# Rounded matrix products whose moving operand is read as two interleaved streams

## The chip, the cores and the metric

The kernel runs on one core of one Trainium2 chip. The metric is device time of one execution in microseconds (us), lower being better. A core has TensorE for matrix products (PE in the rows, with its weight loads as PEld), VectorE (DVE), ScalarE (ACT), GpSimd (POOL) and SyncE (SP), whose queue issues all of this kernel's transfers.

## The reference

What is computed is causal attention with a decay bias, for 8 batches of 8 heads, 576 tokens and 64 features a head, and a gated MLP on the concatenated heads:

```python
scores = q @ k.T / 8                                   # (8, 8, 576, 576)
cum = np.cumsum(np.maximum(s, 0.0), axis=-1)
scores = np.where(causal, -1e9, scores + np.minimum(-(cum[..., :, None] - cum[..., None, :]), 0.0))
attn = np.exp(scores - scores.max(-1)); attn /= attn.sum(-1) + 1e-9
x = heads_concatenated(attn @ v)                       # (8, 576, 512)
h = gelu_tanh(x @ w_in)                                # (8, 576, 1024)
u, v = h[..., :512], h[..., 512:]
v_n = (v - mean(v)) / sqrt(var(v) + 1e-6) * g_ln
v_s = einsum('ts,bsd->btd', w_sg, v_n) + b_sg[None, :, None]
out = x + (u * v_s) @ w_out
```

All tensors are float32.

## The kernel before

Everything is one stream of small instructions that the program first records and then issues in a fixed order: each call goes through a recorder (class `Plan`), and a table of ranks (`RANK`, a packed string) sets the place of every operation on its engine. So all rows of the profile have the recorder's line, and operations are told apart by tile names. A second set of tables (`ALT`, with `ENG` as the default) says for each copy, split and scaling whether ACT (`s`), POOL (`g`) or DVE (`v`) does it. Engines run their own queue strictly in that order.

Products. Most run as rounded float32 (float32r): an operand is split into a rounded high part and a low rest, and a product is the sum of three products (high with high, high with low, low with high) in the same PSUM bank. Each matmul instruction loads 128 columns of weights (the stationary operand) and then streams the columns of the moving operand past them.

- Keys (`qk_part`, tiles `pss<-k,q`): for the 56 heads from number 8 on, the moving operand is a stretch of the split keys `k1`, `k2`; per head two instructions each of 448, 64, 320 and 192 columns and four of 288. Rows 64 and 65 of `k2` hold the running sum `cum` of the bias, brought from a scratch tensor in DRAM. The first 8 heads use unrounded float32 (tiles `kq`, `arena`).
- MLP, for each of 8 batches: `v_unit` (tiles `psm<-wi,xs`, 512 columns of the weights `wi` move; 56 instructions a batch), `u_unit` (`psm<-xs,wi`, 288 token columns of `xs` move; 8 units of 12), `s_unit` (`psm<-ws,vn` and `psm<-wr,vnr`, 288 columns of `ws` move; 8 units of 14), `o_unit` (`psm<-gt,wo`, 288 columns of `gt` move; 8 units of 12). Some go to banks named `pss` or `psp`.
- Transposes of the attention matrix (`psp<-ident,p`) and context products (`psp<-pT,vf`) in unrounded float32.
- At the start `WARM` and `FILL` instructions, which multiply a single column of ones, broadcast to 512 columns (`psm<-wt`), keep TensorE occupied.

Evictions. `gelu2` reads a unit's PSUM bank three times: ACT squares it, DVE reads it twice. The end of `o_unit` reads it once on DVE and adds the residual `xr`. In the key part, `split_k` turns the loaded `raw` into `k1` (copy, `kh`) and the rest (subtraction, `kl`), and SP then moves pieces between partitions.

Of the kernel before, what the change touches and what calls it, by code (L numbers as in the profile page):

```python
# [12 lines left out]
F32 = mybir.dt.float32  # L13
# [52 lines left out]
ENG = dict(kh="s", kl="g", xh="g", xl="g", gh="s", gl="g", wh="s", wl="g", wsh="s", wsl="gggv", n="g", vl="g", ev="s",  # L66
# [4 lines left out]
    "na": "sgggggssgvvgsggsssggvgggsgsggggg",  # L71
    "wh": "svsvsgggsggg",
    "wl": "gggggggggggg",
    "ea": "vvvssvss",
    "xva": "vsss",
    "xa": "ggsgsgss",
    "xal": "gggggggg",
    "nb": "ggsggsggsgssggggggvgvggg",
    "eb": "ssssssss",
    "eb1": "ssssssvv",  # L80
    "xvb": "sssv",
    "rt": "ggvvvggggvgvgvvvgvggvgvvggvvgvggvggvvvvvvvgggggvgvgggggvggvgggggvvgggvvggvgvvvgv",
    "vl": "gggggvgggvggvvgvgvvgggvvgggggggg",
    "kh": "sgsssssvgggvsssggvggvgvgvvsvsgssgssgsgsggvsvsssgssvgggvg",
    "kl": "gggggggvvggggvvgggvvvvgvgggggggvggggvvgvvvvgvvvgvvggggvg",
    "wsh": "sssssssssvsv",
    "wsl": "gggggggvgggg",
    "n": (
        "ggggggvggggggggggggssvggsggssggsssgvgsggsgssgvvsvvgvsgsggvvgsgsvgsvssvvvgssgsggvgsggsgsssssgsgsgvgss"
        "ggvgssggvgggvssgvggsvgvvgsvvsgggvgsssggggssgsgvvgsvgsvgggsgssvgggvsssgvggvggsvvvvgsssgsgsvvssvvvvvgv"  # L90
        "gvvvgvgggsgggssvggggvsvsgsgsgvssvvsvsgsvvvvsggsssgvgggsgsggsssssggvgsgvggssggvggssssvggssgggsgvsvvss"
        "gggsggvvvsgsgvggggggsvggsvsggssgvvsgssvgvvsvvvvsvvggvvsgvvggsggssggssggggssggssssvgsggvggvvg"),
    "ev": (
        "ssvsvsvvvssssvsvssvsssvsssssvsssvsssvvvsvsvvssssvssvsvvsvsssssvsssssssssssssssvvssvsvvssssvsvssvsssv"
        "svsvvvssvvvs"),
    "ev1": "sssvssvsvsvvvvvssssvssssvsvvsvsvssvsvssvssvssvvsssvvsvss",
    "xv": "vsvvvssvssvsvsvsvvsssvssvsvv",
    "xw": "svsvvvvsssssvssvssvvvsssssvs",
    "xz": "sssssvssvvsvsvsvsvsvvvsvsssv",
    "gh": "vgvggvvsgvgssvsggsgsvvsvgvvvgsggvgggvsssgsgsvssgsvgggssgvsvsgggv",  # L100
    "gl": "vvgvvvggvgvvggvgvvgvgvgvgvvvvgggggggggggggggggvggggggggggggvvggv",
    "xh": "ssvssssvgggssvssssssssgvsvvs",
    "xl": "vggvvvvggggggvvvgggvvvvvvgvv",
# [15 lines left out]
    "To!H%H-xXk6XA;hL`U2z>=W(_?}eMf17W4GMz||H6@Cc61wj-=T~x#x!V&?BMTIlMdEt}rU68~;48_FaA>oqnO86|i6MhMgh1bG20f}5pB&HVAh#AC8;yvNHkWS1l"
    "78KtK{{%xMA`=scy@V}-CYmA@<BF-o^kQZ)ub4y3BQ_KM2(svjk(g2}Am$VcizP)@Od`$}vWmIILSkvLf>=$gDApHN3;D$oVqLL=kX`sI)Dr87EyS*3e{rbzLD(<s"  # L120
    "6dH@I#L_}OvA9@9%q12P&k09`Q$i}CoLEJyFSZuji=D-uVkfbII9{ACE)pAwrNl~NbuqcvR~#aa6{m>v#7$xov9{P$Y%U%XJ_>JymSP*RoKREjAa)Z6iX+5v;v{jD"
    "*hQQ#t`gUX-NkldZ!t#fCvFx8h`q$YVpXxBI7mD!4iis_7saDutT<AfAkGn2itEHZ;#P5tI8mG{E*4jd+r{1D0r7;mOFS=L7vqVQ#be?*@xJ&*{3Ze^zIa@`Azl#^"
    "io?ZO;s!CPI9XgMrV!hT&BQEXQSqv{T-+h<70-%K#dqRs@uOHw{3Rkul}3vz#Es%kahe!NGsOMkNpZHAL|P`U6}O4|#3SMv@t*ix{32cxe~P|zLChwW7kh}0#l+Gf"
    "@v?YZd?|hw|A@9ENKeExQYPt{m_SM;WszQqm&9A*L-DP6Q+y$|6W)uT#IIrs>4*4F^du(5k&;P?r1;WbQIRYOOI(U4C6&@j>7{H^ekp@gQ)(hLl<tUk#mrJ+sigEk"
    "d?cDuD8-dTDVbPSOe<y->xdo2nPO#0l61+DWGS)GNNOWNsj1XT(j-H2rPNYZDYsNksv^~rYD*0yB2g)l5=tqhj8bc9kTgQ-BD9b?NZF-MQeP>j)J#e)<&fG+xuhCm"
    "9;twoS1K(Pm5NLKg$h!2sf1KYDkN2v>PY>i;nEmshBR3!BbAk^N%f?bQah==v{+gzZIU`lQ^h6X0&%IhUOXtC7C(purD9TNX^+%Z>Lt~ex=6#MKGGzqo77y2mF7qT"
    "rEyXZsi$;K>MivV(@FWHB2szjn6v{7kbaAmq{h-<DMlJ9jhDWQ-KDA0JZZVKMfxWVk<LhCrMc2lX@j&~x+dL|_DQ>?3({d}uQXFyA{~-0N+YE$;wY(xv{Bk29gt2)"
    "C&71cReCComL^F3r2EoqX`-}Fx+y)AK1$!Eta532iZo4{E`5;F0tNh%>Pq{ilhOidg|tjsEp3$!O1GuW(rjssv`acJot9QgN2K%8dTE<fQ93H!k<LojrCHKtX})wy"
    "dL+G-zDj>24`c?(L1K^wFpv-|lom-lrB%{9>5C+ROOg$~Nx4BG@KE|I)dwNy0Io<kq+8Nm>4EfEdLq4)-b*he1LOo1!2^(5ehG5OucZ8-G^hqDfH%@}>9h1(`Xm7m"
    "7bF2cBoXK!0P#UekOdS3H9#|v5A*;7fech201OfU7sLSwv;ZdfDRGbjK;Qri_<#TkA`lNG0_j0gkPM^(*+CId4m1ayKp)Tzv;)&Xd(a<b1%*K=P#H7?twAr)7YqVj"  # L130
# [1279 lines left out]
def _layout(i):  # L1410
# [9 lines left out]
    def bits(a):  # L1420
        return np.ascontiguousarray(a).view(np.int64) if a.dtype == np.float64 else a
# [39 lines left out]
```

## Time and profile before

| | |
|---|---|
| time, median of 3 runs | 736.41 us (735.29 to 737.32) |
| time of the profiled execution | 735.24 us |
| span in its profile, first to last instruction | 733.5 us |
| TensorE busy | 725.5 us, 99% |
| VectorE, ScalarE, GpSimd busy | 582.0 us (79%), 501.7 us (68%), 367.4 us (50%) |
| granted TensorE clock | 1.000 of full speed on average |

The profiled execution is 1.7 us longer than its span and 1.2 us shorter than the median. A matmul's duration in the rows contains a tail that overlaps the next instruction: many of 288 columns last 299 ns each and start every 133 ns. A rate is therefore read from a run of like instructions in the timeline: the time of the run, less one duration, over one instruction fewer.

### The profile page before, as it was taken

The page shows a single profiled execution, that of the slowest core. Times are in us where ns is not written, and L with a number is a line of the kernel's source. Part 1 is how long each engine was busy: PE and PEld are TensorE (multiplying, and loading weights), DVE is VectorE, ACT ScalarE, POOL GpSimd, SP SyncE. Part 2 cuts the span into 40 slices and gives each one's busy share as a digit, 9 for nine tenths or more (in the row PEclk, how much of TensorE's full clock was granted, in tenths as well). Part 3 has the DMA queues.
Part 4 walks back from the last instruction along what each step waited for, and adds up shares of the span by engine and source line. Part 5 has one row for each costly group of instructions (what it writes and reads, how often), then busy time and mean ns, then how long its engine had stood idle before and what let it go on. Part 6 is the DMA issues. An engine that isn't in the chain of part 4 may idle for free.

```text
span 733.5 us, 16206 instructions
## 1 busy us (share of the span) xinstructions
PE 725.5 (99%) x5337; PEld 641.5 (87%) x5337; DVE 582.0 (79%) x1761; ACT 501.7 (68%) x1378; POOL 367.4 (50%) x604
## 2 busy tenths in 40 slices
PE   8999999999999999999999999999999999999998
PEld 7877789988889888898889898998889888889998
DVE  6898988799887779779897588867898777965663
ACT  5899986777986567855686687866788555931430
POOL 6899897444663344733343263363535454541621
PEclk9999999999999999999999999999999999999999
DMA  8974744555454453353443544434445343100101
GB/s 250 273 197 130 179 124 120 157 142 149 124 157 119 119 136 96 94 155 107 132 123 83 152 122 110 112 96 128 128 132 132 103 120 107 44 9 24 49 17 65
DMA packets 59272, 88.35 MB, mean 120 GB/s; under 512 B 16306, under 2 KB 33972, under 8 KB 59188
## 3 DMA queue, kind: packets, MB, share of 16 engines
q1 hardware_dynamic: 59188, 87.32, 43.5%
q8 instruction: 42, 0.69, 0.4%
q14 instruction: 42, 0.34, 0.2%
HBM read 41.37 MB, written 9.73 MB: 70 GB/s over the span
## 4 chain that ended last, share of the span: by engine, by line
PE 92%; DVE 3%; DMA 2%; ACT 1%; issue 1%; POOL 1%; SPq 0%; DVEq 0%; ACTq 0%; POOLq 0%
PE psm L451 54%; PE psp L451 21%; PE pss L451 16%; DVE p L451 1%; DMA pair<-in_w_in 1%; DMA q<-k 1%; DVE psm L451 1%; DMA k<-cum 0%; POOL p L451 0%; DMA vf<-in_vp 0%; ACT p L451 0%; SPq L451 0%; DVE u L451 0%; DVE vt L451 0%; POOL wi L451 0%
## 5 line engine op out<-in xcount | busy, mean ns | idle before, releaser
L451 ACT ACTIVATE p<-p,mn 128x448 f32<-128x448 f32 (+4 forms) x310 | 172.4, 557 | 49.2 <-DVE mn L451 47.1
L451 DVE CUSTOM_DVE_ANT_0 p<-pss,mask 64x64 f32<-64x64 f32 (+4 forms) x304 | 123.0, 424 | 24.2 <-PE pss L451 20.7
L451 POOL TENSOR_SCALAR p<-p,rs 64x64 f32<-64x64 f32 (+4 forms) x199 | 94.9, 486 | 67.3 <-DVE rs L451 51.5
L451 PE MATMUL psm<-gt,wo 128*128 128x288 f32 x720 | 124.1, 299 | 0.0
L451 PE MATMUL pss<-k,q 128*128 128x288 f32 (+9 forms) x672 | 121.1, 297 | 0.5 <-DVE mn L451 0.4
L451 PE MATMUL psm<-xs,wi 128*128 128x288 f32 x720 | 119.0, 300 | 0.9 <-DVE u L451 0.8
L451 PE MATMUL psm<-ws,vn 128*128 128x288 f32 x708 | 117.4, 298 | 0.0
L451 PEld LDWEIGHTS pss<-k,q 128*128 128x128 f32 (+3 forms) x672 | 102.0, 180 | 9.4 <-DVE mn L451 0.8
L451 PEld LDWEIGHTS psm<-gt,wo 128*128 128x128 f32 x720 | 105.1, 188 | 2.5 <-DVE u L451 0.2
L451 PE MATMUL psm<-wi,xs 128*128 128x512 f32 (+1 forms) x380 | 106.4, 402 | 0.0
L451 PEld LDWEIGHTS psm<-xs,wi 128*128 128x128 f32 x720 | 102.0, 188 | 2.6 <-DVE u L451 1.1
L451 PEld LDWEIGHTS psm<-ws,vn 128*128 128x128 f32 x708 | 101.0, 188 | 1.0
L451 PE MATMUL psp<-pT,vf 128*64 128x64 f32 (+3 forms) x752 | 90.4, 388 | 0.6 <-DVE pT L451 0.6
L451 PEld LDWEIGHTS psp<-pT,vf 128*64 128x64 f32 x752 | 46.6, 137 | 43.7 <-issue 30.5
L451 ACT COPY pT<-psp 128x512 f32<-128x512 f32 x124 | 68.8, 580 | 15.4 <-PE psp L451 15.0
L451 PEld LDWEIGHTS psm<-wi,xs 128*128 128x128 f32 (+1 forms) x380 | 66.6, 184 | 12.9 <-issue 0.6
L451 PE MATMUL psp<-ident,p 128*128 128x128 f32 x744 | 72.4, 247 | 0.0
L451 PEld LDWEIGHTS psp<-ident,p 128*128 128x128 f32 x744 | 70.2, 140 | 2.5 <-issue 0.6
L451 ACT ACTIVATE p<-p,rs 64x64 f32<-64x64 f32 (+4 forms) x138 | 62.8, 475 | 11.0 <-DVE rs L451 7.1
L451 POOL TENSOR_TENSOR k<-raw,k 128x576 fp32r<-128x576 f32 x34 | 48.6, 1430 | 29.0 <-DVE k L451 14.4
L451 POOL TENSOR_TENSOR gt<-u,gt 128x288 fp32r<-128x288 f32 (+1 forms) x44 | 37.4, 854 | 48.5 <-DVE gt L451 25.5
L451 DVE SCALAR_TENSOR_TENSOR u<-u,psm 128x288 f32<-128x288 f32 x120 | 52.5, 442 | 10.1 <-ACT u L451 9.6
(158 smaller groups left out, 1208.2 us busy)
## 6 DMA issues: line engine op xcount, KB each, us to landing
q<-k SPq DMA_DIRECT2D x168, 144.0 KB
raw<-in_kq SPq DMA_DIRECT2D x56, 288.0 KB
vf<-in_vp SPq DMA_DIRECT2D x56, 192.0 KB
out_t<-u SPq DMA_DIRECT2D x64, 144.0 KB
k<-k SPq DMA_DIRECT2D x56, 144.0 KB
pair<-in_w_in SPq DMA_DIRECT2D x8, 512.0 KB
u<-xs SPq DMA_DIRECT2D x32, 64.0 KB
pair<-in_w_out SPq DMA_DIRECT2D x4, 512.0 KB
```

What stands on the lines that cost most here:

```text
L451: fn(*args, **kw)
```

## The change

The moving operand of every rounded product is read through a pattern of three levels, in which the innermost level has two elements far apart: column 0, then column n/2, then 1, then n/2+1 (`woven`), and for keys the same inside groups of eight columns (`woven8`: 0, 4, 1, 5, 2, 6, 3, 7). Where the data comes from DRAM it is stored there in the order that makes the products come out straight: keys in groups of 8, the v half of `w_in`, the columns of `w_sg` and `b_sg`. Where the data is made on the chip (`xs` in `u_unit`, `gt` in `o_unit`), the columns lie interleaved in PSUM, and the readers of PSUM go through it with a step of two (`plain`) and write the two halves apart (`halves`). A second running sum, `cum8`, is made in the order of the keys by one more copy (`c8`) and one more transfer to DRAM; the first 8 heads go on reading `cum`.

The planner's price of a rounded product with such a pattern changes, and the ranks and the tables of engines are new.

```diff
+ENG = dict(c8="g", kh="s", kl="g", xh="g", xl="g", gh="s", gl="g", wh="s", wl="g", wsh="s", wsl="gggv", n="g", vl="g", ev="s",
...
-    "kl": "gggggggvvggggvvgggvvvvgvgggggggvggggvvgvvvvgvvvgvvggggvg",
+    "kl": "gggggggvgggggggggvvggggggggggggvggvggvgggggvggggvvggvggv",
...
+def _view(t, *dims):
+    return bass.AP(t.tensor, t.offset, [list(t.ap)[0]] + [list(x) for x in dims])
+def woven(t):
+    n = _cols(t)
+    return _view(t, (1, n // 2), (n // 2, 2))
+def woven8(t):
+    return _view(t, (8, _cols(t) // 8), (1, 4), (4, 2))
+def plain(t):
+    return _view(t, (1, 2), (2, _cols(t) // 2))
+def halves(t):
+    return t.rearrange("p (a n) -> p a n", a=2)
+def weave(n, k):
+    return np.arange(n).reshape(n // k, k // 2, 2).transpose(0, 2, 1).ravel()
...
-            o.pes.append((max(54.0, 0.836 * w), 0.4397 * n + 6.4, 165.0, 0))
+            fast = list(ins[1].ap)[-1][1] == 2
+            o.pes.append((max(54.0, 0.836 * w), n / 2.4 + 2.6 if fast else 0.4397 * n + 6.4, 165.0, 0))
...
+    c8 = moe.tile([P, S], F32, name="c8", tag="xs", bufs=4)
+    copy("c8", c8.rearrange("p (g b a) -> p g b a", b=2, a=4), _view(cc.bitcast(F32), (8, S // 8), (1, 2), (2, 4)))
+    nc.sync.dma_start(out=cum8.rearrange("a h s -> (a h) s"), in_=c8)
...
-        nc.sync.dma_start(out=k2[64:66, :].bitcast(F32), in_=cum[:, h, :])
+        nc.sync.dma_start(out=k2[64:66, :].bitcast(F32), in_=cum8[:, h, :])
...
-        nc.tensor.matmul(o, d["q1"][:, i0:i0 + r], d["k1"][:, j0:j1], start=True, stop=False)
-        nc.tensor.matmul(o, q2[h % 2][:, i0:i0 + r], d["k2"][0:66, j0:j1], start=False, stop=True)
+        nc.tensor.matmul(o, d["q1"][:, i0:i0 + r], woven8(d["k1"][:, j0:j1]), start=True, stop=False)
+        nc.tensor.matmul(o, q2[h % 2][:, i0:i0 + r], woven8(d["k2"][0:66, j0:j1]), start=False, stop=True)
...
-                        nc.tensor.matmul(ps[0:r], xs[c][:, xi, ts_], wi[:, c, wj, fs],
+                        nc.tensor.matmul(ps[0:r], xs[c][:, xi, ts_], woven(wi[:, c, wj, fs]),
...
-                    nc.tensor.matmul(ps[:, 0:CH], wi[:, c, wj, dt * P:(dt + 1) * P], xs[c][:, xi, cs],
+                    nc.tensor.matmul(ps[:, 0:CH], wi[:, c, wj, dt * P:(dt + 1) * P], woven(xs[c][:, xi, cs]),
...
-            gelu2(ps[:, 0:CH], t)
+            gelu2(plain(ps[:, 0:CH]), halves(t))
...
-                    nc.tensor.matmul(ps[:, 0:CH], vn[j][:, vi, ds_], ws[:, j, wj, cs],
+                    nc.tensor.matmul(ps[:, 0:CH], vn[j][:, vi, ds_], woven(ws[:, j, wj, cs]),
...
-                    nc.tensor.matmul(ps[:, 0:CH], wo[:, c, wj, ms], gt[ch, c][:, gi, :],
+                    nc.tensor.matmul(ps[:, 0:CH], wo[:, c, wj, ms], woven(gt[ch, c][:, gi, :]),
...
-            nc.vector.scalar_tensor_tensor(out=t, in0=ps[:, 0:CH], scalar=0.5, in1=xr[(b, mt)][:, cs],
+            nc.vector.scalar_tensor_tensor(out=halves(t), in0=plain(ps[:, 0:CH]), scalar=0.5, in1=halves(xr[(b, mt)][:, cs]),
...
-    kq = np.concatenate([k.transpose(0, 2, 1), q.transpose(0, 2, 1)[:, :, tok]], axis=1)
+    kq = np.concatenate([k.transpose(0, 2, 1)[:, :, weave(S, 8)], q.transpose(0, 2, 1)[:, :, tok]], axis=1)
...
-        "w_in": bits(i["moe_w_in"]),
+        "w_in": bits(i["moe_w_in"][:, np.concatenate([np.arange(DH), DH + weave(DH, DH)])]),
...
-        "w_sgt": i["moe_w_sg"][tok][:, tok].T,
+        "w_sgt": i["moe_w_sg"][tok[weave(S, CH)]][:, tok].T,
```

The new order at three places. The first is the start of SP's queue, in the loads before the first heads: `cum` is the running sum, `xs_86` and `xs_87` the tile that it comes from, `kb`, `ka`, `vp` and `va` are keys, queries and values, `pair` the raw weights. Before:

```order
L451 DMA e_71<-in_va 128x512 x2
L451 DMA g_b_92<-in_g_ln 128x512
L451 DMA cum<-xs_86 128x576
L451 DMA e_71<-in_va 128x1024
L451 DMA pair_121<-in_w_in 128x1024
L451 DMA vf_140<-in_vp 128x320
```

And now:

```order
L481 DMA e_71<-in_va 128x512
L481 DMA arena_80<-in_kb 64x832
L481 DMA cum<-xs_87 128x576
L481 DMA vf_138<-in_vp 128x320
L481 DMA cum_76<-xs_88 128x576
L481 DMA e_71<-in_va 128x1024
```

One transfer of 128x576 is added (`cum_76` is `cum8`, from the copy `xs_88`, which POOL makes), two places behind `cum`; the weights' loads stand elsewhere.

The second place is the split of the keys of head 22. Before, DVE makes the low part (`k_291<-raw_355`) between two score evictions (`ISA p<-pss`) and the statistics of a v unit (`rt`):

```order
L451 SCALAR_TENSOR_TENSOR u_295_367<-u_295_367,psm_65 128x288
L451 ISA p_66,mn_350<-pss_59,mask_18_90,mn_350 128x288
L451 ISA mn_350 128x1
L451 TENSOR_TENSOR k_291_363<-raw_355,k_290_362 128x576
L451 SCALAR_TENSOR_TENSOR rt_360<-rt_360 128x1
L451 TENSOR_SCALAR rt_360<-rt_360 128x1
L451 TENSOR_TENSOR rt_360<-rt_360 128x1
L451 COPY pT_24_96<-psp_61 128x512
```

Now POOL makes the same low part (`k_292<-raw_357`), between scalings of attention rows and that statistics chain:

```order
L481 TENSOR_SCALAR p_68<-p_68,rs_339 64x64
L481 TENSOR_TENSOR k_292_365<-raw_357,k_291_364 128x576
L481 TENSOR_SCALAR rt_362<-mv_361 128x1
L481 TENSOR_TENSOR rt_362<-rt_362,few_93 128x1
L481 TENSOR_SCALAR p_66<-p_66,rs_356 128x320
L481 TENSOR_TENSOR rt_362<-rt_362 128x1 x2
```

Over the whole program the low parts of keys go from 22 on DVE and 34 on POOL to 11 and 45.

The third place is PE's queue at that head's first products. Before, keys of 320 and 192 columns stand between two units of 288 and then come v products of 512:

```order
L451 MATMUL psm_65<-xs_316,wi_99 128x288 x2
L451 MATMUL psm_65<-xs_320,wi_99 128x288 x3
L451 MATMUL pss_59<-k_290_362,q_292_364 128x320
L451 MATMUL pss_59<-k_291_363,q_0_25_97 128x320
L451 MATMUL pss_59<-k_290_362,q_292_364 128x192
L451 MATMUL pss_59<-k_291_363,q_0_25_97 128x192
L451 MATMUL psm_64<-xs_307,wi_99 128x288 x2
L451 MATMUL psm_64<-xs_311,wi_99 128x288
L451 MATMUL psm_63<-wi_99,u_310_382 128x512
```

Now:

```order
L481 MATMUL psm_65<-xs_318,wi_101 128x288
L481 MATMUL psm_65<-xs_322,wi_101 128x288 x3
L481 MATMUL pss_59<-k_291_364,q_293_366 128x320
L481 MATMUL pss_59<-k_292_365,q_0_26_99 128x320
L481 MATMUL pss_59<-k_291_364,q_293_366 128x192
L481 MATMUL pss_59<-k_292_365,q_0_26_99 128x192
L481 MATMUL psm_64<-xs_309,wi_101 128x288 x3
L481 MATMUL psm_64<-xs_313,wi_101 128x288 x3
L481 MATMUL psm_64<-xs_318,wi_101 128x288 x3
```

The kinds, shapes and numbers of TensorE's instructions are the same over the whole program (4867 in the program's list, both times); only what stands beside what has moved.

## Rows read from the trace of the kernel before

**Rows 1.** The page, span and busy time of each engine.

```profile
span 733.5 us, 16206 instructions
...
PE 725.5 (99%) x5337; PEld 641.5 (87%) x5337; DVE 582.0 (79%) x1761; ACT 501.7 (68%) x1378; POOL 367.4 (50%) x604
```

**Rows 2.** The page's chain that ended last, shares by engine.

```profile
PE 92%; DVE 3%; DMA 2%; ACT 1%; issue 1%; POOL 1%; SPq 0%; DVEq 0%; ACTq 0%; POOLq 0%
```

**Rows 3.** Longest wait of PE: tile, releaser, us in total, times, longest.

```profile
PE psm L451 <- DMA kq<-in_ka: 1.6, 1, 1.6
```

**Rows 4.** Windows: us, busy PE, PEld, DVE, ACT, POOL, clock, DMA share, GB/s.

```profile
0.00:20.00 20.00, 17.35 (x87) 14.59 (x88) 14.15 (x50) 10.79 (x34) 13.32 (x31) 1.00 0.89 263
100.00:200.00 100.00, 99.17 (x756) 87.75 (x755) 86.45 (x274) 78.70 (x223) 54.83 (x76) 1.00 0.51 137
200.00:300.00 100.00, 99.74 (x750) 88.60 (x749) 82.78 (x264) 71.72 (x202) 45.55 (x76) 1.00 0.47 127
...
400.00:500.00 100.00, 100.00 (x743) 89.98 (x742) 75.11 (x238) 72.71 (x197) 42.01 (x71) 1.00 0.43 116
```

**Rows 5.** Timeline of PE: start, us to last end, tile, shape, count.

```profile
683.55 1.79 PE L451 MATMUL pss<-wi,xs 128*128 128x512 f32 x7
685.18 3.36 PE L451 MATMUL psm<-gt,wo 128*128 128x288 f32 x24
...
4.73 2.57 PE L451 MATMUL psm<-wt 128*128 128x512 f32 x11
...
275.78 0.27 PE L451 MATMUL pss<-k,q 66*128 66x192 f32 x1
275.89 0.32 PE L451 MATMUL psm<-gt,wo 128*128 128x288 f32 x1
```

**Rows 6.** PE groups by form (last: us 5.1 to 7.0): count, busy us, mean ns.

```profile
L451 PE MATMUL psm<-gt,wo 128*128 128x288 f32 x720 | 124.1, 299 | 0.0
...
L451 PE MATMUL pss<-wi,xs 128*128 128x512 f32 x24 | 6.9, 395 | 0.0
...
L451 PE MATMUL psm<-wt 128*128 128x512 f32 x11 | 2.6, 381 | 0.0
```

**Rows 7.** The chain in order of time, us 414: start, us, what.

```profile
414.09 2.85 PE psp L451 x24
```

**Rows 8.** Groups of DVE and ACT by form that read PSUM.

```profile
L451 DVE SCALAR_TENSOR_TENSOR u<-u,psm 128x288 f32<-128x288 f32 x120 | 52.5, 442 | 10.1 <-ACT u L451 9.6
...
L451 DVE SCALAR_TENSOR_TENSOR u<-psm,xr 128x288 f32<-128x288 f32 x60 | 27.0, 453 | 21.8 <-PE psm L451 21.1
...
L451 DVE SCALAR_TENSOR_TENSOR vt<-vt,psm 128x512 f32<-128x512 f32 x29 | 19.7, 678 | 4.6 <-ACT vt L451 4.5
...
L451 DVE SCALAR_TENSOR_TENSOR gt<-pair,psm 128x512 int32<-128x512 int32 x12 | 8.2, 680 | 0.1
...
L451 ACT ACTIVATE u<-psm 128x288 f32<-128x288 f32 x60 | 24.1, 404 | 23.7 <-PE psm L451 23.4
```

**Rows 9.** Groups of DVE and POOL that split keys.

```profile
L451 DVE TENSOR_TENSOR k<-raw,k 128x576 fp32r<-128x576 f32 x22 | 17.7, 804 | 4.2 <-ACT k L451 4.1
...
L451 POOL TENSOR_TENSOR k<-raw,k 128x576 fp32r<-128x576 f32 x34 | 48.6, 1430 | 29.0 <-DVE k L451 14.4 <-ACT k L451 9.2 <-DMA vf<-in_vp 3.0
...
L451 POOL TENSOR_SCALAR k<-raw 128x576 fp32r<-128x576 f32 x21 | 14.3, 681 | 40.9 <-PE pss L451 33.8 <-DMA k<-k 2.7 <-PE psm L451 1.8
```

**Rows 10.** The chain in order of time, us 79 to 87: start, us, what.

```profile
79.11 4.75 DMA q<-k
...
83.88 2.92 DMA k<-cum
```

**Rows 11.** Timeline of the end: start, us, what, [idle before].

```profile
729.02 1.23 PE L451 MATMUL psm<-gt,wo 128*128 128x288 f32 x8
...
730.28 0.46 DVE L451 SCALAR_TENSOR_TENSOR u<-psm,xr 128x288 f32<-128x288 f32 x1 [0.61 <-PE psm L451]
```

More of the change, by code (lines that the diff above doesn't have):

```diff
@@ L70 @@
     "th": "s",
[L71 to L78, printed above, removed]
+    "c8": "g",
+    "na": "sggsggssgvvgsggggggsvgggsgssgggs",
+    "wh": "sgsgvsgssggg",
+    "wl": "vggvgggggggg",
+    "ea": "svvssvss",
+    "xva": "ssss",
+    "xa": "ggggggss",
+    "xal": "vggggggg",
+    "nb": "ggsggsggssssggvgggvgvggg",
     "eb": "ssssssss",
-    "eb1": "ssssssvv",
+    "eb1": "ssvsssvv",
@@ L81 @@
     "xvb": "sssv",
[L82 to L86 removed]
+    "rt": "gggvgggggvgvvvggggvvvggggggggvggvgvvgvvvgvvvgvgvgvgggggvggvggvgvvggvggvvggvggvgv",
+    "vl": "gggggvgggvggvvvggggggvvvvvvgggvg",
+    "kh": "sgsssssssggsgsssgsggvsvsggsssvvgvgssggvsvgsgvssgggvvggvs",
@@ L102 @@
-    "xh": "ssvssssvgggssvssssssssgvsvvs",
-    "xl": "vggvvvvggggggvvvgggvvvvvvgvv",
+        "ssvsssvvvsvsvsvvssvsssvsssssssssssssvvsvvssvsssssvsvvvsvsvsssssvvsvvssvvsssvsssssvsvvvssssvsvsvsssvs"
+        "svsvssssssss"),
+    "ev1": "ssvvsssssssvvvvvsssssssvvvsssvsvssvvvsssvssssvvssvsvsvsv",
+    "xv": "sssssvssvvssssvvsssvssssvsvs",
+    "xw": "vssvsssvsvvssvsvsvsvvvvsssvs",
+    "xz": "ssvsssvvsvvsssvsssssvssssvvv",
+    "gh": "vssvvsvsgvsssvgvggvssggsgsvvvvsvvggsggssgssssgssvvgsvvgsvgggvvvs",
@@ L104 @@
+    "gl": "vgvgggggvvggggvgvvgggvgvggvggvvggvvvvggvvgvggvgvggvvggvvgggvvvgg",
+    "xh": "sgvvssssgssgvssgsvsgsssgggsg",
+    "xl": "vvgvvggvggvgvvvvgvgvgvggvggv",
 }
@@ L119 @@
[L119 to L130, printed above, removed]
@@ new lines @@
+    "^Nc(*&%(3woIDTD%M0>CyfDA-J@rcS>byR0&MWdtygdKwDcs@_Pr#G%OuQCP#hdb!JU6extMS!d4PKk);%Rv{UWeD?4R~YTgg4`@c?aH`59XuzBtD(b<tz9szLy{2"
+    "{dj*qkPqT9d>r4%XYvJn2p`IaahnG`KKFTIo}ZWC!}$n4nvdZV_+;LWx94qmPaey=^8vgg@60I=c|2a1H{xA*SKf{H;JtVs-j|Q%6ZsUrmha-L`5L~CPvwjFCcc?x"
+    "<y(0xzKU<-hxloJhri?(`DK2CU*I?S4xWtf<a_u&zMmiDC-^mfkH6(#_%Hs4%f97{KKJAM)A$TNo6q6%_<X*QFXl`5Qofvj<k0`kfAW=lJ>Sg_^JRPs-_AGi1N=O{"
+    "%a8J7{5U_!Pw_MSI)A|5@caA;Kg-YY<o+don}6b8x#P$4ukfq<7Jtq^^Y1(jugXXA@tpd$@A|$U_>upPdwyI$fuGb*>8J5C`dR#femTFM-^6d`xAq(Ref%+gtpAWF"
@@ L238 @@
+    "qk2(;sBzRK>Kb*6x<~z@A<=*7d}|>")
 N3 = 8
@@ L1202, in v_unit @@
                     if c < 3:
-                        nc.tensor.matmul(ps, xq[c], wi[:, c, 0, fs], start=(c == 0), stop=False)
+                        nc.tensor.matmul(ps, xq[c], woven(wi[:, c, 0, fs]), start=(c == 0), stop=False)
                         yield W5
-                    nc.tensor.matmul(ps[0:r], xs[c][:, 0, ts_], wi[:, c, 1, fs], start=False, stop=False)
+                    nc.tensor.matmul(ps[0:r], xs[c][:, 0, ts_], woven(wi[:, c, 1, fs]), start=False, stop=False)
                     yield W5
                     if c == 3:
-                        nc.tensor.matmul(ps, xq[c], wi[:, c, 0, fs], start=False, stop=True)
+                        nc.tensor.matmul(ps, xq[c], woven(wi[:, c, 0, fs]), start=False, stop=True)
                         yield W5
@@ L1288, in s_unit @@
                     n += 1
-            nc.tensor.matmul(ps[:, 0:CH], vn[4][:, ds_], wr1[:, cs], start=False, stop=False)
+            nc.tensor.matmul(ps[:, 0:CH], vn[4][:, ds_], woven(wr1[:, cs]), start=False, stop=False)
             yield W2
-            nc.tensor.matmul(ps[:, 0:CH], vnr2[:, ds_], wr2[:, cs], start=False, stop=True)
+            nc.tensor.matmul(ps[:, 0:CH], vnr2[:, ds_], woven(wr2[:, cs]), start=False, stop=True)
             yield W2
```

250 lines of the change are left out of this document (125 added, 125 removed).

## The prediction

> **What bounds the kernel now.** I read the page's busy times first: TensorE is busy 99% of the span, VectorE 79%, ScalarE 68%, GpSimd 50% [rows 1]. A busy TensorE need not be at its peak, so the chain that ended last came next: 92% of it lies on TensorE [rows 2]. Its longest wait for another engine is 1.6 us, at the start [rows 3], and in the windows from 100 us on it is busy 99 to 100 us of each 100 [rows 4]. The exception is the stretch before 87 us, where the chain runs partly through transfers (4.75 and 2.92 us in one place, [rows 10]). So the time is the sum of what TensorE streams, and the question is what a column costs it.
>
> The timeline answers that. Seven products of 512 columns take 1.79 us [rows 5] with a last duration of 0.395 [rows 6]: (1.79 - 0.395) / 6 = 232.5 ns each. Twenty-four of 288 take 3.36 us, the last 0.299: 3.061 / 23 = 133.1 ns. The two widths give the price of a column, 99.4 / 224 = 0.444 ns, and of an instruction, 133.1 - 288 x 0.444 = 5.3 ns. [...]
>
> **The change, part by part.** *Reads in two streams.* From the loops of the program: 8 batches x (96 u + 112 s + 96 o) = 2432 instructions of 288 columns and 224 of keys; 448 of 512; and 112 each of 448, 320, 192 and 64. Together 3552 instructions and 1.109 million columns, so each 0.01 ns of a column is 11 us of the kernel. No row shows a rounded product with such a pattern. [...] The loss side stands under the rivals.
>
> [...]
>
> *Can the weight loads follow?* A full weight load stands before each product. Behind a 192-column key product the next product of 288 starts after 0.11 us [rows 5], so a load needs no more than that; 133 - 10 = 123 ns stays above it. [...]
>
> *Reads of PSUM with a step of two.* 64 u units are read twice by VectorE (442 ns) and once by ScalarE (404), 64 o units once by VectorE (453) [rows 8]. Unknown in PSUM. The nearest rows are VectorE's reads of the raw weights, every second word in SBUF: 680 ns against 678 for the plain form of that size [rows 8]. From above: if each of the 288 elements took a second turn at the rate of those rows ((678 - 442) / 224 = 1.05 ns), 303 ns more, 192 x 0.303 = 58 us of VectorE. I take 0 by the nearest row; VectorE's slack hides some of it, and the upper end is a rival below. At the end, one such read lies bare behind the last product (0.46 us, [rows 11]): 0.3 us at most.
>
> *The second running sum.* One POOL copy of 128x576, 0.68 us by its plain twin [rows 9], and one transfer of 0.29 MB. Behind the copy POOL has memsets, and SP's queue the values and weights of the first heads; the transfers there move 263 GB/s [rows 4], so they come about 1.1 us later. Its reader is head 8, whose running sum lands at 86.8 us now [rows 10]. TensorE's own work for the first heads covers it; without that cover, 1.1 us.
>
> *The new order.* TensorE has the same instructions. Eleven low parts of keys leave VectorE (11 x 0.80 = 8.8 us) for POOL (11 x 1.43 = 15.7 us) [rows 9]; POOL is half idle after 100 us [rows 4] and hides them. What is behind them on POOL is the statistics chain of a v unit and scalings of attention rows, which come up to 1.4 us later and whose readers have other units' products in front of them.
>
> *What is late next.* The other engines must do the same work in 5% less time. VectorE's fullest window, 86.5 of 100 us [rows 4], less 1.2 for the moved keys, becomes 85.3 of 95, 90%. I allow 1.5 us for new waits there and 1.5 for the 28 us or so before 87 us in which the chain is not TensorE's, where about 5% of the stretch is not gained: 3 us.
>
> **Sum.** On the profiled execution's own time: 735.2 - 36.4 + 3 = 701.8 us. The median lies 1.2 above that execution: 703.
>
> **Rivals.** *Each read of a new place waits, and the kernel is slower.* Neighbouring columns of the moving operand now come from two places 576 to 1024 bytes apart (16 bytes for keys). If TensorE's reader holds one piece of SBUF at a time, every column fetches anew what contiguous reading fetched once for several. The start-up row, with no walking at all, doesn't exclude it, and no row has an alternating read. It decides as soon as a column costs above 0.446 ns, 0.5% more than now. At the slowest column of any row, the unrounded context products with 24 instructions over 3200 columns in 2.85 us [rows 7], 0.89 ns, the loss is 1.109 million x 0.446 = 495 us: about 1230 us. [...]
>
> [...]
>
> *VectorE becomes the bound.* With 303 ns more for each of 192 reads, some 30 of them per 100 us, VectorE would have 85.3 + 9.1 = 94 of 95 us in the fullest window and 91 in the next, 83 in the loosest [rows 4]. An in-order engine that full holds up TensorE; if three of six windows lose what they gained (5 us each), 718 us. For it speaks only that no strided read of PSUM is shown; against it, the strided rows of SBUF.
>
> **How the numbers follow.** My forecast, with its own range of 691 (all the fixed part gone) to 710 (none of it, and some more waits): 0.72. VectorE the bound: 0.10, 712 to 726. Nothing in the rate: 0.08. Slower by the reads: 0.10. The range of 692 to 724 holds nearly all of the first and most of the second. About 0.3% either way (2.2 us) is what a measurement of this kernel can tell. Faster: 0.72 + 0.10 + 0.02 of the third case = 0.84; the same 0.05; slower 0.10 + 0.01.
>
> **What will show it.** A run of 24 products of 288 should take 3.14 us (123.6 ns each) and seven of 512 1.70 us; with the fixed part whole 3.18 and 1.71, and with no effect 3.36 and 1.79. The start-up products and the context products must keep their times. The u and o reads should stay at 442 and 453 ns; at 700 or more the third rival is on. TensorE should stay at 98 to 99% of a span near 700, VectorE rise to about 82%. I am wrong if the runs don't shorten, if keys (groups of eight) behave unlike the wide patterns, or if the runs shorten and the windows fill with waits for VectorE.

## The result, and the profile after

| | before | after |
|---|---|---|
| time, median | 736.48 us (4 runs, 735.29 to 737.32) | 709.51 us (4 runs, 707.96 to 709.99) |
| ratio to before | | 0.9631, 95% interval 0.961 to 0.9652 |
| span of the profiled execution | 733.5 us | 707.9 us |

The change takes 27 us away. The forecast was 703, with a range of 692 to 724. The page of the changed kernel, span, busy times and shares of the chain that ended last:

```profile
span 707.9 us, 16218 instructions
...
PE 694.4 (98%) x5337; PEld 617.7 (87%) x5337; DVE 573.8 (81%) x1732; ACT 506.2 (72%) x1398; POOL 366.8 (52%) x612
...
PE 83%; DVE 7%; ACT 4%; POOL 2%; DMA 2%; issue 1%; SPq 0%; DVEq 0%; POOLq 0%
```

TensorE's busy time fell by 31.1 us [rows 1], the span by 25.6: the difference, 5.5 us, is new idle time, and the chain is on TensorE for 83% now instead of 92% [rows 2]. First the rate. Timeline of PE after, two runs of like products (start, us, tile, shape, count):

```profile
649.38 1.67 PE L481 MATMUL psm<-wi,xs 128*128 128x512 f32 x7
661.43 2.74 PE L481 MATMUL psm<-gt,wo 128*128 128x288 f32 x21
```

Groups by form after, for PE, DVE and ACT (count, busy us, mean ns):

```profile
L481 PE MATMUL psm<-gt,wo 128*128 128x288 f32 x720 | 118.0, 289 | 0.0
...
L481 PE MATMUL pss<-wi,xs 128*128 128x512 f32 x24 | 7.2, 379 | 0.0
...
L481 DVE SCALAR_TENSOR_TENSOR u<-u,psm 128x288 f32<-128x288 f32 x120 | 52.8, 444 | 11.1 <-ACT u L481 10.3
L481 DVE SCALAR_TENSOR_TENSOR u<-psm,xr 128x288 f32<-128x288 f32 x60 | 27.1, 452 | 14.5 <-PE psm L481 14.2
...
L481 ACT ACTIVATE u<-psm 128x288 f32<-128x288 f32 x60 | 24.0, 404 | 12.4 <-PE psm L481 8.7 <-DVE gt L481 3.6
```

A product of 288 columns now starts every (2.74 - 0.289) / 20 = 122.6 ns instead of 133.1, one of 512 every (1.67 - 0.379) / 6 = 215 instead of 232.5 [rows 5, 6]. PSUM read with a step of two costs nothing here: 444 and 452 ns on VectorE and 404 on ScalarE, against 442, 453 and 404 [rows 8].

By these rates the shorter stream is worth 39 us, an estimate: 2432 x 10.5 ns = 25.5, 448 x 17.3 ns = 7.8, and 5.7 for the keys (median distance of like neighbours in the two traces: 134 to 126 ns at 288 columns, 205 to 190 at 448, 148 to 136 at 320, 93 to 85 at 192, the same at 64). The span fell by 25.6, so 13.4 us were lost: 5.5 as the new idle time, the rest in stretches in which TensorE counts as busy. Where, the windows show (us, busy and instructions of PE, PEld, DVE, ACT, POOL, clock, DMA share, GB/s). Before:

```profile
0.00:120.00 120.00, 115.57 (x810) 95.18 (x811) 102.00 (x321) 98.24 (x283) 101.87 (x173) 1.00 0.68 185
120.00:700.00 580.00, 579.71 (x4304) 516.30 (x4301) 464.11 (x1404) 398.48 (x1085) 259.24 (x421) 1.00 0.41 112
```

After:

```profile
0.00:120.00 120.00, 110.76 (x766) 90.91 (x767) 101.36 (x303) 95.48 (x273) 92.69 (x166) 0.99 0.67 180
120.00:700.00 580.00, 578.91 (x4537) 522.27 (x4536) 470.58 (x1425) 410.67 (x1127) 273.31 (x446) 1.00 0.43 114
```

From 120 us on TensorE gets through 5% more products in the same time. In the first 120 us it gets through 44 fewer than before. A mark makes this exact: the first product of the first `o_unit`, `psm<-gt,wo`. Instructions of that tile in a window (count, least/median/most ns, first and last start), before and after:

```profile
L451 PE MATMUL psm<-gt,wo x60: 292/296/398, 121.9 to 157.3; 128*128 128x288 f32 x60
```

```profile
L481 PE MATMUL psm<-gt,wo x54: 283/286/369, 128.3 to 159.2; 128*128 128x288 f32 x54
```

From the mark to the end it takes 733.5 - 121.9 = 611.6 us before and 579.6 after: 32.0 of the stretch's 35.7 us are kept. Up to the mark it takes 6.4 us more, although 3.3 us less is streamed there (164 MLP products of 288 columns and 56 of 512, and six heads' keys).

Two things happen in that first stretch. Waits of PE after (tile, releaser, us in total, times, longest):

```profile
PE psm L481 <- DVE gt L481: 2.8, 2, 2.2
PE psm L481 <- DVE u L481: 2.1, 2, 1.6
```

Timeline of PE after, us 12 to 17:

```profile
12.34 0.38 PE L481 MATMUL psm<-wt 128*128 128x512 f32 x1
14.88 0.66 PE L481 MATMUL psm<-kq 128*128 128x64 f32 x4 [2.16 <-DVE gt L481]
...
15.46 1.62 PE L481 MATMUL pss<-arena 128*128 128x320 f32 x4
```

Timelines of DVE and of ACT after, around 12 us:

```profile
12.67 0.70 DVE L481 TENSOR_SCALAR psm<-psm 128x512 int32<-128x512 int32 x1 [3.31 <-ACT psm L481]
```

```profile
12.01 0.63 ACT L481 ACTIVATE psm<-pair 128x512 f32<-128x512 f32 x1 [5.59 <-DMA pair<-in_w_in]
```

The same step of ACT before:

```profile
9.39 0.63 ACT L451 ACTIVATE psm<-pair 128x512 f32<-128x512 f32 x1 [3.06 <-DMA pair<-in_w_in]
```

And its transfer in the chains in order of time (start, us, what), before and after:

```profile
2.63 6.73 DMA pair<-in_w_in
```

```profile
3.91 8.08 DMA pair<-in_w_in
```

In both orders ScalarE decodes the first weights ahead of the first heads' exponentials. What differs is their transfer: in the new order it is the sixth in SP's queue instead of the fourth, starts 1.3 us later and lands 2.6 us later. ScalarE, then VectorE, then TensorE wait for it in turn. Behind that wait TensorE's granted clock is 0.50 of full speed in each window of 1 us from 16 to 19, and 0.66 on average from 15 to 20: four products of 320 columns, the first at 15.46, take 1.62 us, against 1.11 at a clock of 1.00 in fill_start below. The window after (columns as above):

```profile
15.00:20.00 5.00, 5.00 (x21) 4.24 (x22) 2.85 (x14) 4.53 (x17) 0.34 (x2) 0.66 0.98 229
```

### The profile page after: what moved, and what is told of

It is laid out like the page before. It is cut to its first block, busy times and chain, and to the rows that moved or that the text cites. A ratio compares the mean times of both kernels' runs of the same rounds, so it can differ in the third digit from the quotient of the medians.

```text
span 707.9 us, 16218 instructions
## 1 busy us (share of the span) xinstructions
PE 694.4 (98%) x5337; PEld 617.7 (87%) x5337; DVE 573.8 (81%) x1732; ACT 506.2 (72%) x1398; POOL 366.8 (52%) x612
## 4 chain that ended last, share of the span: by engine, by line
PE 83%; DVE 7%; ACT 4%; POOL 2%; DMA 2%; issue 1%; SPq 0%; DVEq 0%; POOLq 0%
PE psm L481 49%; PE psp L481 20%; PE pss L481 14%; DVE p L481 2%; ACT p L481 1%; DMA pair<-in_w_in 1%; DVE psm L481 1%; DVE u L481 1%; DVE gt L481 1%; DVE rt L481 1%; ACT vt L481 0%; POOL p L481 0%; ACT pT L481 0%; ACT psm L481 0%; DMA raw<-in_kq 0%
## 5 line engine op out<-in xcount | busy, mean ns | idle before, releaser
L481 ACT ACTIVATE p<-p,mn 64x64 f32<-64x64 f32 (+4 forms) x310 | 172.0, 556 | 33.7 <-DVE mn L481 31.5
L481 DVE CUSTOM_DVE_ANT_0 p<-pss,mask 128x448 f32<-128x448 f32 (+4 forms) x304 | 121.5, 423 | 24.6 <-PE pss L481 19.2
L481 PE MATMUL psm<-gt,wo 128*128 128x288 f32 x720 | 118.0, 289 | 0.0
L481 PE MATMUL pss<-k,q 128*128 128x288 f32 (+9 forms) x672 | 115.1, 290 | 1.5 <-DVE mn L481 1.1
L481 PE MATMUL psm<-xs,wi 128*128 128x288 f32 x720 | 112.8, 291 | 0.5 <-DVE u L481 0.5
L481 PE MATMUL psm<-ws,vn 128*128 128x288 f32 x708 | 111.1, 289 | 1.6 <-DVE u L481 1.6
L481 PEld LDWEIGHTS pss<-k,q 66*128 66x128 f32 (+3 forms) x672 | 98.2, 181 | 8.3 <-DVE mn L481 2.1
L481 PE MATMUL psm<-wi,xs 128*128 128x512 f32 (+1 forms) x380 | 98.7, 385 | 0.7 <-DVE gt L481 0.7
L481 POOL TENSOR_TENSOR k<-raw,k 128x576 fp32r<-128x576 f32 x45 | 65.1, 1447 | 43.9 <-ACT k L481 26.5
L481 ACT ACTIVATION_READ_ACCUMULATOR p<-p,mn 128x1 f32 (+1 forms) x310 | 58.7, 189 | 0.0
```

What stands on the lines that cost most here:

```text
L481: fn(*args, **kw)
```

## Experiments

**Order and reads taken apart.** The new reads with the tables of engines and ranks of before; and the new order with the reads, layouts and evictions of before. (The changed lines are given in short form; `c8` of old_order_woven takes its buffer from the pool of `xr`.)

```diff
# old_order_woven
-ALT, RANK = those of the changed kernel
+ALT, RANK = those of the kernel before; the two new operations (c8) follow the one that is recorded ahead of them
# new_order_plain
-        nc.tensor.matmul(..., woven(ws[:, j, wj, cs]), ...)      # all uses of woven, woven8, plain, halves, weave
+        nc.tensor.matmul(..., ws[:, j, wj, cs], ...)
```

> The changed reads, layouts and evictions in the order and with the engines of before; the second running sum is added right behind the first (one copy and one transfer). Products stream 38 us less than before (2656 x 10.6 ns, 448 x 16, narrower keys the rest). Theory that the new order brings the waits (TensorE waits some 8 us more than before, most of it ahead of 125 us): 699 to 703 us, faster than the changed kernel. Rival that the shorter stream brings them, since the other engines can't follow it: 707 to 716 us.

> The changed kernel's order and engines with contiguous reads and the old layouts and evictions (the second running sum is still copied and brought, now in plain order). Theory that the new order brings the waits: all 38 us of stream come back and the waits stay, 745 to 749 us, slower than before by over 1%. Rival that the shorter stream brings them: with longer products the waits close, 735 to 741 us. If reads had nothing to do with the gain: 710 us.

Measured: 707.17 us (ratio 0.9605, interval 0.958 to 0.9629) and 741.04 us (1.0068, 1.0045 to 1.009). The first says that the shorter stream brings most of the waits whatever the order, the second lies at the upper end of the rival's range. Against the 735.67 us that the kernel before took beside them, the reads make the gain, 28.5 us in the old order and 31.5 in the new, and the new order by itself costs 5.4. The old order with woven reads is no slower than the changed kernel. Up to the mark and from it to the end, with the other runs:

| kernel | mark, us | from the mark to the end, us | granted clock, 0 to 120 us |
|---|---|---|---|
| before | 121.9 | 611.6 | 1.00 |
| new_order_plain | 130.4 | 611.4 | 0.97 |
| old_order_woven | 122.9 | 582.6 | 1.00 |
| after | 128.3 | 579.6 | 0.99 |
| fill_start | 126.0 | 579.7 | 1.00 |
| mlp_woven_only | 130.4 | 583.5 | 0.97 |
| keys_woven_only | 124.2 | 607.3 | 1.00 |
| spliced | 124.0 | 581.4 | 1.00 |

With plain reads the two orders are equal behind the mark. With woven reads the new order is 3 us better there, and 5.4 us worse ahead of it. There its first wait for `gt` makes a difference from run to run: 0.6 us of it in keys_woven_only, 2.7 in mlp_woven_only, 3.0 in new_order_plain. Each row is one execution, the profiled one, and the longer waits go with a lower clock (2.7 and 3.0 us with 0.97, 0.6 us with 1.00). The other executions of new_order_plain, at a mean clock of 1.000, took 739.4 to 741.2 us and the profiled one 743.7; of mlp_woven_only two at 1.000 took 710.3 and 711.1 and the profiled one 715.9. So the marks of 130.4 stand some us later than in those.

**The clock behind the wait.** Nine more products of the column of ones where TensorE waited at 12.7 us.

```diff
     for i in range(FILL):
         nc.tensor.matmul(wm, wt.broadcast_to([P, P]), wt.broadcast_to([P, 512]), start=True, stop=True)
+        if i == 18:
+            # nine more of them, next to this one in the order
```

> The changed kernel with 9 more start-up products where TensorE now waits 2.16 us (12.7 to 14.9 us), behind which the granted clock shows half speed for 3.4 us. If the wait brings the half clock: the clock stays at full speed, TensorE does in those 3.4 us twice as much, 707 to 708.5 us. If the clock falls whatever stands there, or the stretch has slack for it: 709.5.

Measured: 708.6 us (0.9629, 0.9608 to 0.9651), between the two forecasts. Timeline of PE in this kernel:

```profile
12.22 2.35 PE L492 MATMUL psm<-wt 128*128 128x512 f32 x10
...
14.88 1.11 PE L492 MATMUL pss<-arena 128*128 128x320 f32 x4
```

In this execution the granted clock is 1.00 from 15 to 20 us, where it was 0.66, and the mark comes 2.3 us earlier; the medians differ by 0.9 us, which the intervals do not separate. In another of its four executions the mean clock was 0.995, below all four of the changed kernel (0.997 and 0.998), and where in it the clock fell no trace shows. By the mark the clock is a part of the start's loss, 2.3 us, and not most of it.

**Keys and MLP apart**, in the new order: keys plain, MLP woven; and the reverse.

```diff
# mlp_woven_only
-        nc.tensor.matmul(o, d["q1"][:, i0:i0 + r], woven8(d["k1"][:, j0:j1]), start=True, stop=False)
+        nc.tensor.matmul(o, d["q1"][:, i0:i0 + r], d["k1"][:, j0:j1], start=True, stop=False)
```

> The new order with plain keys and woven MLP products. The stream of the MLP is 2432 x 10.5 ns and 448 x 17 ns shorter, 33 us of 38.4. Theory that each part keeps the share that the whole kept (31.5 of 38.4, 0.82): 741.0 - 27.2 = 714 us. Rival, the waits of other engines swallow what is shortened last, so that the keys add little: 709 to 711.

> The new order with woven keys and plain MLP products: 5.3 us less to stream. Theory of an equal share: 741.0 - 4.3 = 736.7 us. Rival, keys stand in a chain of splits, transfers and evictions that sets their time, and gain nothing: 740 to 742. Rival, early savings are kept whole and only the last are swallowed: 735.7.

Measured: 713.51 us (0.9683, 0.9637 to 0.9729) and 735.42 (0.9991, 0.9973 to 1.0008). Against new_order_plain the parts gain 27.5 and 5.6 us, both together 31.5. The times alone do not decide: the interval of mlp_woven_only reaches 3.4 us to either side, and its executions fall in two pairs, 710.3 and 711.1, at the upper end of the rival's range (709 to 711), and 715.9 and 716.1; keys_woven_only lies nearest to 735.7, the forecast of early savings kept whole. Behind the mark, where the clock is full, the parts gain 27.9 of 30.6 and 4.1 of 5.1 us, and both together 31.8: there they add up, and nothing is swallowed because it came last. (The 38.4 us of these expectations used slightly shorter distances than the 39 above.)

**The old start with the new rest.** Ranks and engines of the old tables for every operation up to about 255 us, those of the new tables from there (the rule by which the tables were made, not lines of the kernel).

```diff
+E = place_in_old_order < 2750
+rank = argsort(argsort(where(E, place_in_old_order, 100000 + place_in_new_order)))
```

> Woven reads everywhere; the order and the choice of engines of the old table up to about 255 us, and of the new table from there (at the seam 8 operations of 6793 stand on different sides, one product among them). Theory that the new order loses its 6 us in the first 255 us and earns in the rest by itself, where the old order fills with waits: 709.5 - 6 = 703.5 us (702.5 to 704.5). Rival, the lead of the old order is borrowed, and the other engines, which must do the same work, take it back after the seam: 707 to 710.

Measured: 705.85 us (0.9594, 0.9569 to 0.9619), between the two: of the 6 us some 3.7 stay. The mark came at 124.0, and the rest took 581.4, so the lead is neither wholly local nor wholly borrowed. Of the kernels that leave nothing out this has the lowest median; the intervals do not separate it from old_order_woven.

**What holds the first 122 us: engines or transfers?** Two suspects, each taken away alone and both together, in the old order with woven reads (mark 122.9).

```diff
# light_plain (on the kernel before), light_woven (on old_order_woven): less work ahead of the mark
-                             accum_out=sums[pslot(h)][0:r, it:it + 1])
+                             **({} if h < SPL + 2 else dict(accum_out=sums[pslot(h)][0:r, it:it + 1])))
+            if it and h < SPL + 2:
+                o[0] = o[0][0][:, 0:64], o[0][1][:, 0:64], o[0][2]
-        nc.vector.tensor_scalar(out=b, in0=b, scalar1=3, scalar2=None, op0=ALU.logical_shift_left)
+        nc.vector.tensor_scalar(out=b[:, 0:64], in0=b[:, 0:64], scalar1=3, scalar2=None, op0=ALU.logical_shift_left)
# half_woven (on old_order_woven), light_half_woven (on light_woven): half of each weight transfer
-        nc.sync.dma_start(out=raw.rearrange("p n a -> p (n a)"), in_=src.bitcast(I32))
-        l32, h32 = raw[:, :, 0], raw[:, :, 1]
+        nc.sync.dma_start(out=raw[:, 0:n], in_=src.bitcast(I32)[:, 0:n])
+        l32, h32 = (_view(raw[:, i:i + 1], (0, 2), (2, n // 2)) for i in range(2))
```

> The kernel before, with work taken from VectorE, ScalarE and GpSimd in the first 120 us alone: the sums of the first ten heads' exponentials are not read out (they stay 1), their rows are scaled in the first 64 columns only, and two of the four steps that decode the wide weights run on 64 of 512 columns. The output is therefore not that of the reference; TensorE does the same. It is the control of light_woven. In the kernel before, the first product of psm<-gt,wo starts at 121.9 us, and TensorE idles 4.4 us before 130 us. Theory that the three other engines are as full as TensorE there: the marker falls by what TensorE waited for them and no more, to 119 to 121 us, and the time to 733 to 735 us. Rival, transfers and latencies set that stretch: 121.5 to 122.5 and no change of the time.

> The same work taken from the old order with woven reads, whose marker is at 122.9 us and whose time is 707.2 us. Theory that the shorter stream of the first 120 us (4 us less) was lost to engines that were already full: with that work gone the marker falls by the 4 us and by the waits, to 116 to 118 us, 3 us or more earlier than in light_plain, where it is 1.0 later now; time 701 to 703 us. Rival, transfers and latencies: the marker stays at 121.5 to 123 and the time at 706 to 708.

> The old order with woven reads, in which each of the 12 wide transfers of weights brings half of its bytes (0.26 MB instead of 0.52) and the decode reads that half twice, so that the output is not that of the reference; instructions, order and TensorE's work stay. Theory that the transfers of the start bind the first 122 us: the marker, the first product of psm<-gt,wo, falls from 122.9 to 120 to 121.5 us and the time from 707.2 to 704.5 to 706. Rival, single chains of small transfers, of their issue in SP's queue and of a v unit's statistics set the stretch, and bytes do not matter: 122.3 to 123.3 and 706.5 to 708.

> Both at once: the transfers of the weights halved and the work of VectorE, ScalarE and GpSimd in the first 120 us lightened as in light_woven (marker 122.7, time 706.2). Theory that engines and transfers bind in turns, so that only both together let the shorter stream show: marker 117.5 to 120.5 and 702 to 704 us. Rival as before, chains of latency: 122 to 123 and 705.5 to 707.

| kernel | time, us | ratio, interval | mark, us | from the mark, us |
|---|---|---|---|---|
| light_plain | 735.38 | 0.9988, 0.9977 to 0.9998 | 121.2 | 612.5 |
| light_woven | 706.2 | 0.9592, 0.9569 to 0.9616 | 122.7 | 583.1 |
| half_woven | 703.38 | 0.9557, 0.9541 to 0.9573 | 119.2 | 582.1 |
| light_half_woven | 702.38 | 0.9542, 0.9527 to 0.9556 | 117.7 | 582.9 |

My own theory, that the other three engines were full ahead of the mark, fell as it stood: in light_woven VectorE, ScalarE and GpSimd do 92.7, 93.3 and 93.0 us of work in the first 120 instead of 100.8, 97.9 and 101.0, and the mark comes at 122.7, not at 116 to 118. The clock has a part in that. Behind a wait of 1.9 us for the transfer `u<-xs` it fell; the window of 58 to 62 us:

```profile
58.00:62.00 4.00, 4.00 (x20) 3.21 (x18) 1.35 (x4) 1.92 (x4) 3.92 (x7) 0.57 0.68 205
```

That is some 1.7 us of work (an estimate: 0.43 x 4 us), and the mark would stand near 121 without it, still short of the theory; the fastest of the four executions took 703.86 us, where the theory wanted 701 to 703. The chain of light_woven in order of time (start, us, what) runs through transfers:

```profile
33.63 7.53 DMA pair<-in_w_in
41.17 6.81 DMA q<-k
48.84 2.92 DMA q<-k
...
53.34 3.50 DMA u<-xs
```

That of its control, light_plain, runs through products up to 51.6 us and then through the same last transfer, for which TensorE waits 0.6 us there:

```profile
52.36 3.67 DMA u<-xs
```

With half the weights' bytes and the work left whole, the mark comes 3.7 us earlier and the time falls by 3.8. In the chain of old_order_woven three transfers stand between 28 and 122 us, 16.5 us in all (8.72, 4.99 and 2.80), between stretches of the other engines; in that of half_woven none. Instructions of the tile in half_woven:

```profile
L491 PE MATMUL psm<-gt,wo x63: 283/286/390, 119.2 to 160.0; 128*128 128x288 f32 x63
```

So with woven reads in the old order the bytes of the start hold that stretch, and by more than forecast. Lighter engines give 1.0 us by the medians with whole and with halved bytes alike, which the intervals do not separate from nothing; at the marks it is 0.2 us, under the lower clock, and 1.5. That they help only once the bytes are halved is not shown. The halving was not run with plain reads, so how much of the 3.7 us the kernel before would also gain stays open.

**The read by itself.** Blocks of 40 products back to back, each with another read order of the moving operand (levels as step, count, innermost last; the notes behind the lines are not in the kernels).

```diff
+    ("mb", 288, ((1, 144), (144, 2))),             # woven: 0, 144, 1, 145
...
+    ("md", 288, ((2, 144), (1, 2))),               # three levels, straight order
+    ("me", 576, ((2, 288),)),                      # every second word
+    ("mf", 1152, ((4, 288),)),                     # every fourth word
+    ("mg", 288, ((4, 72), (1, 2), (2, 2))),        # 0, 2, 1, 3
+    ("mh", 288, ((1, 72), (72, 4))),               # four streams
...
+    ("mk", 288, ((0, 288),)),                      # one column, again and again
...
+    ("mm", 288, ((2, 72), (144, 2), (1, 2))),      # 0, 1, 144, 145
...
+    ("nc", "r", 288, ((1, 144), (1, 2))),          # 0, 1, 1, 2, 2, 3
...
+    ("ne", "r", 578, ((2, 144), (289, 2))),        # two far streams, each in steps of two
+    ("nf", "r", 576, ((4, 144), (1, 2))),          # 0, 1, 4, 5
```

> A kernel that leaves out all of the computation and writes zeros: after a warm-up, 16 blocks of 40 rounded products with one set of weights, all of 288 columns but the last two (512), each block reading its moving tile in another order. Contiguous (ma) should start every 133 ns and woven halves (mb) and woven eights (mc) every 122 to 124, as in the two profiles. Theory of two streams (what matters is that neighbours come from two places): the same three-level form in straight order (md) stays at 133; pairs two words apart (mg: 0, 2, 1, 3), pairs 64 bytes apart (mi), four streams (mh) and six (ml) run at 122 to 124; adjacent pairs from two places (mm: 0, 1, 144, 145) in between. Rival of the form (the innermost level of two is what matters, in whatever order): md too at 122 to 124. Rival of the line (each access to a new piece of SBUF costs): a single stream with a step of 4 words (mf) or 16 (mj) far slower than 133, 240 or more, and mb slower than mc; if mf and mj stay at or below 133, a new line costs nothing by itself. One re-read column (mk): 122 to 125.

> Eleven blocks of 40 rounded or other products of 288 columns, each with another read order of the moving operand; the kernel computes nothing of the reference and writes zeros. [...]

Timeline of PE in reads_alone (start, us of the whole block):

```profile
29.06 5.43 PE L82 MATMUL ps<-ma,w 128*128 128x288 f32 x40
34.33 5.06 PE L82 MATMUL ps<-mb,w 128*128 128x288 f32 x40
39.23 5.06 PE L82 MATMUL ps<-mc,w 128*128 128x288 f32 x40
44.13 5.49 PE L82 MATMUL ps<-md,w 128*128 128x288 f32 x40
49.46 10.41 PE L82 MATMUL ps<-me,w 128*128 128x288 f32 x40
59.69 10.63 PE L82 MATMUL ps<-mf,w 128*128 128x288 f32 x40
70.14 5.45 PE L82 MATMUL ps<-mg,w 128*128 128x288 f32 x40
75.43 6.30 PE L82 MATMUL ps<-mh,w 128*128 128x288 f32 x40
81.56 5.07 PE L82 MATMUL ps<-mi,w 128*128 128x288 f32 x40
...
96.32 5.19 PE L82 MATMUL ps<-mk,w 128*128 128x288 f32 x40
...
108.00 7.64 PE L82 MATMUL ps<-mm,w 128*128 128x288 f32 x40
...
120.39 9.53 PE L82 MATMUL ps<-mo,w 128*128 128x512 f32 x40
129.75 8.79 PE L82 MATMUL ps<-mp,w 128*128 128x512 f32 x40
```

And in reads_more:

```profile
29.54 5.43 PE L84 MATMUL ps<-na,w 128*128 128x288 f32 x40
34.81 5.06 PE L84 MATMUL ps<-nb,w 128*128 128x288 f32 x40
39.71 5.06 PE L84 MATMUL ps<-nc,w 128*128 128x288 f32 x40
...
49.51 5.24 PE L84 MATMUL ps<-ne,w 128*128 128x288 f32 x40
54.59 10.49 PE L84 MATMUL ps<-nf,w 128*128 128x288 f32 x40
64.90 7.91 PE L84 MATMUL ps<-ng,w 128*128 128x288 f32 x40
72.64 5.08 PE L84 MATMUL ps<-nh,wb 128*128 128x288 bf16 x40
77.56 11.09 PE L84 MATMUL ps<-ni,wb 128*128 128x288 bf16 x40
88.50 19.56 PE L84 MATMUL ps<-nj,wf 128*128 128x288 f32 x80
107.89 24.52 PE L84 MATMUL ps<-nk,wf 128*128 128x288 f32 x80
```

A block less one product (its mean in the groups, 0.286 to 0.467 us), over 39, is the distance of starts. The mean granted clock is 0.924 in both executions; that of single blocks is not shown, but contiguous and woven blocks come within 1.5 ns of the 133.1 and 122.6 that the kernels before and after take at a clock of 1.00. Contiguous (ma, na) takes (5.43 - 0.294) / 39 = 132 ns and woven (mb, nb; mc in eights) 122. It is not the form, since three levels in straight order (md) take 133. The theory of two streams fell: pairs two words apart (mg) take 132, four streams (mh) 153 and six (ml) 166, where it wanted 122 to 124. The 122 comes with streams 64 bytes apart (mi, in stretches of 16 words) and even with 0, 1, 1, 2, 2, 3 (nc), where nothing lies far apart: so it is not the distance of the two places.

Most blocks can be put in order by a count taken from their read orders alone: take the even positions of the stream and the odd ones apart, and count in each how many successive reads lie in the same four words of the tile. With four the distance is 122 ns (mb, mc, mi, nc); with two, 132 (contiguous, mg) and 127 (ne); with one and a third on average (ng, 0, 1, 3, 4) 193; with one, 256 to 261 (me, nf, mf). The same count over the whole stream does not order them: 0, 1, 4, 5 (nf) and every second word (me) have two successive reads in the same four words and take 258 and 256, and woven columns (mb), which change the four words at every read, take 122.

Three things do not fit. In mh, ml and mm the count is one, as in nf, and they cost less (153, 166 and 187). In ne it is two, as in contiguous reads, and it takes 127. One column read again and again (mk) takes 126, more than woven columns. The count describes these blocks; what in TensorE makes the difference, no run shows.

## Why the prediction came out as it did

- **The column.** Right in kind: a woven product of 288 columns starts 10.5 ns sooner behind its neighbour, one of 512 17.3. The size was my estimate: no run shows the least cost of a column, from which the 36.4 us of the sum and the 123.6 ns of the test were worked out. The runs showed 39 us by the rates and 122.6 ns in their place.
- **The fixed part.** I took a third of the 5.3 ns, by the start-up products, which read one column again and again. They were a poor stand-in, since such a column takes 125.7 ns in the blocks (mk) and woven columns 122.4. The gain grows with the columns: 10.5 ns at 288 and 17.3 at 512 are 0.036 and 0.034 ns a column. In the blocks contiguous reads come out at (234.2 - 131.7) / 224 = 0.458 ns a column and nothing fixed, so how the gain divides between column and instruction stays open. Woven takes 122.4 ns at 288 columns and (8.79 - 0.379) / 39 = 215.7 at 512 there, 0.4165 ns a column and 2.4 fixed. By the rates the stream got shorter by 39 us, not 36.4.
- **Reads of PSUM, transfer of the second running sum.** The first cost nothing, as taken (444 and 452 ns on VectorE, against 442 and 453). The second was not run alone; what it costs lies within the 4.3 us that the old order's start loses (a mark 1.0 us later with 3.3 us less to stream).
- **New waits: the step that failed in size.** I allowed 1.5 us for VectorE and 1.5 for the 28 us ahead of 87 us that the chain did not spend on TensorE; 13.4 were lost. Behind the mark 3.7 us are lost. The windows show 0.8 of them as idle time of TensorE (0.3 us before, 1.1 after); the rest are starts that come later than the rate of like neighbours, and no run says why. Ahead of the mark 9.7 are lost: 3.3 of shorter stream that bring nothing, and 6.4 more time. By the mark of old_order_woven 4.3 of them come with the reads in the old order too, and 5.4 with the new order. I took the whole of the rest of the start for TensorE's own, because it was busy there, and did not ask which transfer came next behind it. Halving the weights' bytes gave 3.7 us back in the old order, which points at transfers; without the same run with plain reads it is not shown that they took the 4.3.
- **The new order.** I costed its move of keys and no more. In it the first weights' transfer stands two places further back and lands 2.6 us later, and the wait for it reaches TensorE; that, and the clock of 0.50 behind it, were not in the sum. The clock is 2.3 of the 5.4 us by the mark of fill_start; the transfer was not moved back alone, so that it makes the rest is argued. What the order gives back, 3 us behind the mark, wasn't in the sum either.
- **The rivals.** Slower by a new place at every read: a read order that costs 261 ns exists, a step of four words (mf), but woven columns, of which each lies 576 bytes from the one before (mb), take 122.4, and no block of 288 takes less. No change in the rate: excluded by 122.6. VectorE the bound by PSUM: excluded by 444 and 452 ns.

So the forecast lies 6.5 us below the median by two errors that stand against each other: 2.6 us too little for the stream, 10.4 too little for waits. Between the spans that makes 7.8; between the medians it is less, mainly because I added 1.2 us for a profiled execution below its median, and that of the changed kernel lay 0.45 above. That the time lies in the range is in part luck: with the stream sized right and the same waits I would have forecast 700.

## What to carry to other kernels

For rounded float32, give the moving operand to TensorE as two half streams in turns when the layout of the data can be chosen for nothing (here 122.6 ns instead of 133.1 a product of 288 columns); measure the order of the words in a block of like products first, since it moves the distance of starts between 122 and 261 ns. Do not copy it to other types without that (bf16 in the blocks: 273 ns woven, 123 contiguous). And where the bound engine gets faster, look in each stretch for what arrives just in time now: transfers of the start did not get shorter with the products here (6.73 us for the first weights before, 8.08 after), and an order that put this one further back in the queue made three engines wait for it in turn (5.59, 3.31 and 2.16 us).

## What was not expected of the hardware

- With bf16 the woven order (ni) takes (11.09 - 0.435) / 39 = 273 ns and the contiguous one (nh) 123; with unrounded float32 (two instructions a product in the trace) 304 and 242 ns an instruction (nk, nj). The order that helps rounded products hurts both.
- After the wait of 2.16 us the granted clock was 0.50 of full speed from 16 to 19 us (mean of 0.66 from 15 to 20 us); in the profiled execution with the wait filled it was 1.00 from 15 to 20. In light_woven it fell in the same way behind a wait of 1.9 us (mean of 0.57 from 58 to 62 us).
